# Feed-forward's second product: w_out's high and low parts side by side in one 512-column stream, halves added on eviction, and the bound on |h| found without GpSimd

## The chip, the cores and the metric

The kernel runs on one core of a Trainium2 chip (trn2). The metric is the time of one execution in device microseconds (us); lower is better. Engines: TensorE (PE, its weight loads PEld), VectorE (DVE), ScalarE (ACT), GpSimd (POOL) and the DMA queues (SP's among them).

## The reference, cut to what matters

The kernel computes three layers in turn. Only the last, the feed-forward layer, is touched.

```python
x = fourier_filter(x)                      # 8 x 3072 rows of 256 features -> 24576 tokens
x = mixture_of_experts(x)                  # one expert of 8 per token, 256 -> 1024 -> 256
h = x @ w_in                               # 24576 x 256  @  256 x 2048
g = h - np.tanh(h)
out = g @ w_out                            # 24576 x 2048 @ 2048 x 256, all float32
```

## The kernel before

**Precision.** An operand is split into a high and a low part in a rounded 32-bit format (fp32r, F32R in the code), and a product is the sum of three: high by high, high by low, low by high. x and w_in have parts xh, xl and wih, wil; g has gh, gl; w_out lies in `wo` as 128 x 16 x 2 x 256: for each of 16 blocks f of 128 hidden features first its high part (index 0), then its low part (index 1), 256 columns each.

**Tiling.** `ff_phase` takes the 24576 tokens in NT = 48 tiles of TM = 512, and each tile in 16 steps f. Step f of a tile has these parts:

- `up(X, f)`: six matmuls of 512 columns make h (128 hidden features x 512 tokens) in one PSUM bank of the pool `hp` (4 buffers).
- `small(h)`: ScalarE squares h to u (L1006) and makes s from u (L1007); VectorE makes s = (s + KAPPA) * u (L1008) and g = s * h (L1009). This is h - tanh(h) without its last factor Q3[2], for |h| up to SMALL.
- `parts(g)`: ScalarE rounds g to gh (L998), GpSimd subtracts to gl (L999).
- `down(f, g, po)`: for each of four groups a of 128 tokens three matmuls of 256 columns: gh with wo's high part, gh with its low part, gl with its high part (L1034), each with a weight load of its own. All three add into the same 128 x 256 piece of PSUM. `po` is two tiles of 128 x 2 x 256, a bank each, of the pool `op` (4 buffers), so two token tiles have room.
- after f = 15 `store`: ScalarE copies the two banks to SBUF with the factor Q3[2] (`ob`, L1040), and GpSimd issues four indirect DMAs of 128 rows to the output (L1043), one a step.

**Order.** The order on every engine is that of the program. In turn k of the loop over all 768 (t, f) come `up` and `small` of step k, `parts` of step k-1, then `down` of step k - LAG (LAG = 4), and one pending output DMA. TensorE's order is thus one `up`, one `down`, one `up`, and so on.

**The bound.** The series in `small` holds for |h| up to 0.15. `column_sums` (four times in tile NT-3) adds |w_in| over its two halves. `limit` (before step (NT-2, 0)) sums that over the partitions with four matmuls into buffers of `hp` (L968), takes their maxima on VectorE (L969), reduces them and the maxima of |x| over the 128 partitions on GpSimd (`partition_all_reduce`, L974) and multiplies. If the bound is exceeded, a general loop at the end computes all of it again; with these inputs it is skipped.

Of the kernel before, what the change touches and what calls it, by code (L numbers as in the profile page):

```python
# [16 lines left out]
F32 = mybir.dt.float32  # L17
# [9 lines left out]
D = 256  # L27
# [26 lines left out]
def flat(t):  # L54
    return t.rearrange("p a b -> p (a b)")
# [876 lines left out]
def ff_phase(tc, x2T, ids, out, weights, mx, N, X0):  # L932

    nc = tc.nc
    wih, wil, wo = weights
    NT = N // TM
    with ExitStack() as es:
        P = lambda name, bufs, **kw: es.enter_context(tc.tile_pool(name=name, bufs=bufs, reuse_waits="tile", **kw))
        cp = P("gc", 1)
        beta = cp.tile([128, 1], F32, name="beta")  # L940
        nc.vector.memset(beta, BETA)
        xp = P("gx", 2)
        tp = P("gt", 3)
        hp = P("gh", 4, space=PSUM, side="right")
        op = P("go", 4, space=PSUM)
        one = cp.tile([128, 128], F32, name="gone")
        nc.vector.memset(one, 1.0)
        ones = cp.tile([128, 128], F32R, name="gones")
        nc.scalar.activation(ones, one, AF.Copy)
        big = cp.tile([1, 1], F32, name="big")  # L950
        bigi = cp.tile([1, 1], I32, name="bigi")

        lm = cp.tile([128, 4], F32, name="lm")
        l1 = cp.tile([128, FF], F32R, name="l1")

        def column_sums(q):

            c = slice(TM * q, TM * q + TM)
            a = [cp.tile([128, TM], F32, name=f"abs{k}") for k in range(2)]
            for k in range(2):  # L960
                nc.scalar.activation(a[k], wih[:, k, c].bitcast(F32), AF.Abs)
            nc.vector.tensor_tensor(l1[:, c], *a, op=ALU.add)

        def limit():

            for q in range(4):
                t = hp.tile([128, TM], F32, name="h")
                nc.tensor.matmul(t, ones, l1[:, TM * q : TM * q + TM], start=True, stop=True)  # L968
                nc.vector.tensor_reduce(lm[:, q : q + 1], t, axis=AX.X, op=ALU.max)  # L969
            bound = cp.tile([128, 2], F32, name="bound")  # L970
            nc.vector.tensor_reduce(bound[:, 0:1], lm, axis=AX.X, op=ALU.max)
            nc.vector.tensor_reduce(bound[:, 1:2], mx, axis=AX.X, op=ALU.max)
            allmax = cp.tile([128, 2], F32, name="allmax")
            nc.gpsimd.partition_all_reduce(allmax, bound, 128, bass.bass_isa.ReduceOp.max)  # L974
            nc.vector.tensor_tensor(big, allmax[:1, 0:1], allmax[:1, 1:2], op=ALU.mult)
            nc.vector.tensor_scalar(big, big, 0.99 * SMALL, None, op0=ALU.is_le)
            nc.vector.tensor_scalar(bigi, big, -1.0, 1.0, op0=ALU.mult, op1=ALU.add)

        def load(c):
            steps, X = ff_load(tc, xp, 2, nc.sync, x2T, ids, c)  # L980
            for f in steps:
                f()
            return X

        def up(X, f):
            h = hp.tile([128, TM], F32, name="h")
            c = slice(128 * f, 128 * f + 128)
            n = 0
            for k in range(2):
                for a, b in ((wih, X[0]), (wih, X[1]), (wil, X[0])):  # L990
                    nc.tensor.matmul(h, a[:, k, c], b[:, k], start=n == 0, stop=n == 5)  # L991
                    n += 1
            return h

        def parts(g):
            gh = tp.tile([128, TM], F32R, name="gh")
            gl = tp.tile([128, TM], F32R, name="gl")
            nc.scalar.activation(gh, g, AF.Copy)  # L998
            nc.gpsimd.tensor_tensor(gl, g, gh.bitcast(F32), op=ALU.subtract)  # L999
            return gh, gl  # L1000

        def small(h):
            u = tp.tile([128, TM], F32, name="u")
            s = tp.tile([128, TM], F32, name="s")
            g = tp.tile([128, TM], F32, name="g")
            nc.scalar.activation(u, h, AF.Square)  # L1006
            nc.scalar.activation(s, u, AF.Square, bias=beta)  # L1007
            nc.vector.scalar_tensor_tensor(s, s, KAPPA, u, op0=ALU.add, op1=ALU.mult)  # L1008
            nc.vector.tensor_tensor(g, s, h, op=ALU.mult)  # L1009
            return g  # L1010

        def general(h):
            u = tp.tile([128, TM], F32, name="u")
            s = tp.tile([128, TM], F32, name="s")
            g = tp.tile([128, TM], F32, name="g")
            m = tp.tile([128, TM], I32, name="m", bufs=1)
            t = tp.tile([128, TM], F32, name="t", bufs=1)
            nc.scalar.activation(u, h, AF.Square)
            nc.scalar.activation(t, h, AF.Tanh)
            nc.vector.tensor_scalar(m, u, MID * MID, None, op0=ALU.is_gt)  # L1020
            nc.vector.tensor_tensor(t, h, t, op=ALU.subtract)
            nc.vector.tensor_scalar(u, u, MID * MID, None, op0=ALU.min)
            nc.vector.tensor_scalar(s, u, Q8[7], None, op0=ALU.mult)
            for q in Q8[6::-1]:
                nc.vector.scalar_tensor_tensor(s, s, q, u, op0=ALU.add, op1=ALU.mult)
            nc.vector.tensor_tensor(g, s, h, op=ALU.mult)
            nc.vector.copy_predicated(g, m, t)
            return parts(g)

        def down(f, g, po):  # L1030
            gh, gl = [z.rearrange("p (a n) -> p a n", a=4) for z in g]
            for a in range(4):
                for n, (p, q) in enumerate(((gh, 0), (gh, 1), (gl, 0))):
                    nc.tensor.matmul(po[a // 2][:, a % 2], p[:, a], wo[:, f, q], start=f == 0 and n == 0 and a % 2 == 0,  # L1034
                                     stop=f == 15 and n == 2 and a % 2 == 1)

        def store(ix, po, scale, group):
            ob = [xp.tile([128, 2, D], F32, name="ob", bufs=4) for _ in range(2)]
            for i in range(2):
                nc.scalar.activation(ob[i], po[i], AF.Copy, scale=scale)  # L1040

            def rows(a):
                i = nc.gpsimd.indirect_dma_start(  # L1043
                    out=out, out_offset=bass.IndirectOffsetOnAxis(ap=ix[:, a : a + 1], axis=0),
                    in_=ob[a // 2][:, a % 2], in_offset=None, bounds_check=N - 1, oob_is_err=False)
                if group:
                    tc.declare_no_dep(i.ins, group=group, reason="every token has a row of its own")
                    tc.add_to_no_dep_group(group, i.ins)

            return [lambda a=a: rows(a) for a in range(4)]  # L1050

        seq = [(t, f) for t in range(NT) for f in range(16)]
        X = {0: X0}
        G = {}
        late = []
        LAG = 4
        for k in range(len(seq) + LAG):
            if k < len(seq):
                t, f = seq[k]
                if f == 8 and t + 1 < NT:  # L1060
                    X[t + 1] = load(bass.ds(N - (t + 2) * TM, TM))
                if t == NT - 3 and f % 4 == 2:
                    column_sums(f // 4)
                if (t, f) == (NT - 2, 0):
                    limit()
                G[t, f] = small(up(X[t], f))
            if 0 < k <= len(seq):
                G[seq[k - 1]] = parts(G[seq[k - 1]])
            if k >= LAG:
                t, f = seq[k - LAG]  # L1070
                if f == 0:
                    po = [op.tile([128, 2, D], F32, name="po") for _ in range(2)]
                down(f, G.pop((t, f)), po)
                if f == 15:
                    late = store(X.pop(t)[2], po, Q3[2], "out")
            if late:
                late.pop(0)()
        for f in late:
            f()


        r = nc.values_load(bigi, min_val=0, max_val=1, skip_runtime_bounds_check_because="0 or 1")
        with tc.If(r != 0):
            with tc.For_i(0, N, TM) as i:
                Xi = load(bass.ds(i, TM))
                po = [op.tile([128, 2, D], F32, name="po") for _ in range(2)]
                for f in range(16):
                    down(f, general(up(Xi, f)), po)
                for f in store(Xi[2], po, 1.0, None):
                    f()  # L1090


# [70 lines left out]
```

## Time and profile before

| | us |
|---|---|
| median of 3 runs | 4018.46 |
| lowest and highest run | 4014.62, 4025.91 |
| the profiled execution's own time | 4024.83 |
| its span, first to last instruction | 4023.0 |

The profile records every instruction of one execution. [...] The chain is the work that ended last, followed back from the end. A wait is named by what ended it.

### The profile page before, as it was taken

The page shows a single profiled execution, that of the slowest core. Times are in us where ns is not written, and L with a number is a line of the kernel's source. Part 1 is how long each engine was busy: PE and PEld are TensorE (multiplying, and loading weights), DVE is VectorE, ACT ScalarE, POOL GpSimd, SP SyncE. Part 2 cuts the span into 40 slices and gives each one's busy share as a digit, 9 for nine tenths or more (in the row PEclk, how much of TensorE's full clock was granted, in tenths as well). Part 3 has the DMA queues.
Part 4 walks back from the last instruction along what each step waited for, and adds up shares of the span by engine and source line. Part 5 has one row for each costly group of instructions (what it writes and reads, how often), then busy time and mean ns, then how long its engine had stood idle before and what let it go on. Part 6 is the DMA issues. An engine that isn't in the chain of part 4 may idle for free.

```text
span 4023.0 us, 65752 instructions
## 1 busy us (share of the span) xinstructions
PE 3904.8 (97%) x23204; PEld 3527.1 (88%) x23204; DVE 2621.8 (65%) x4370; ACT 2514.1 (62%) x4318; POOL 2051.7 (51%) x1514
## 2 busy tenths in 40 slices
PE   6899979999999999999999999999999999999998
PEld 3666659999999999999999999999999999999987
DVE  4799986788888877865555555555555555555554
ACT  3455544555555555556777777777777777777775
POOL 2366664344444444444555555555555555555545
PEclk8999999999999999999999999999999999999999
DMA  9898863332333232221000000000001000000000
GB/s 275 264 295 279 270 186 102 76 80 62 77 80 80 55 75 75 54 71 35 22 26 28 22 22 23 26 27 22 22 24 30 22 22 22 26 28 22 22 17 17
DMA packets 297874, 300.13 MB, mean 75 GB/s; under 512 B 158905, under 2 KB 240450, under 8 KB 297538
## 3 DMA queue, kind: packets, MB, share of 16 engines
q1 hardware_dynamic: 275714, 241.83, 21.3%
q0 software_dynamic: 18432, 51.14, 3.5%
q8 instruction: 184, 3.01, 0.3%
q10 hardware_dynamic: 3392, 2.90, 0.2%
q14 instruction: 152, 1.25, 0.1%
HBM read 282.46 MB, written 132.72 MB: 103 GB/s over the span
## 4 chain that ended last, share of the span: by engine, by line
PE 85%; DVE 7%; DMA 4%; issue 2%; POOL 1%; SPq 1%; ACT 1%; POOLq 0%; DVEq 0%; ACTq 0%
PE po L1034 27%; PE h L991 26%; PE h L807 14%; PE o L835 14%; DVE u L261 1%; DVE v L260 1%; DVE v L259 1%; DMA out<-ob,ix 1%; PE z L254 1%; PE z L269 1%; PE z L296 1%; PE L L308 1%; PE z L229 1%; DMA region<-Y,pi 1%; DMA z1d<-a 1%
## 5 line engine op out<-in xcount | busy, mean ns | idle before, releaser
L999 POOL TENSOR_TENSOR gl<-g,gh 128x512 fp32r<-128x512 f32 x768 | 992.9, 1293 | 987.7 <-ACT gh L998 980.4
L1008 DVE SCALAR_TENSOR_TENSOR s<-s,u 128x512 f32<-128x512 f32 x768 | 535.0, 697 | 951.9 <-ACT s L1007 950.1
L1034 PE MATMUL po<-wo,gh 128*128 128x256 f32 x6144 | 1143.0, 282 | 0.0
L1034 PEld LDWEIGHTS po<-wo,gh 128*128 128x128 f32 x6144 | 1007.3, 189 | 71.3
L1034 PE MATMUL po<-wo,gl 128*128 128x256 f32 x3072 | 874.7, 285 | 4.0 <-POOL gl L999 4.0
L1006 ACT ACTIVATE u<-h 128x512 f32<-128x512 f32 x768 | 459.0, 598 | 584.1 <-PE h L991 583.9
L991 PE MATMUL h<-xh,wih 128*128 128x512 f32 x1536 | 610.7, 398 | 0.1
L991 PE MATMUL h<-xl,wih 128*128 128x512 f32 x1536 | 607.6, 396 | 0.0
L991 PE MATMUL h<-xh,wil 128*128 128x512 f32 x1536 | 603.9, 393 | 0.0
L1034 PEld LDWEIGHTS po<-wo,gl 128*128 128x128 f32 x3072 | 581.2, 189 | 4.3 <-POOL gl L999 4.2
L1009 DVE TENSOR_TENSOR g<-s,h 128x512 f32<-128x512 f32 x768 | 529.1, 689 | 84.5 <-POOL gl L999 3.7
L1007 ACT ACTIVATE s<-u,beta 128x512 f32<-128x512 f32 x768 | 554.7, 722 | 25.2
L757 POOL TENSOR_TENSOR w2l<-raw,w2h 128x1024 fp32r<-128x1024 f32 x130 | 349.9, 2692 | 416.7 <-ACT w2h L756 414.4
L817 ACT ACTIVATE hh<-h 128x384 fp32r<-128x384 f32 (+1 forms) x556 | 269.5, 498 | 458.1 <-PE h L807 443.4
L998 ACT ACTIVATE gh<-g 128x512 fp32r<-128x512 f32 x768 | 485.4, 632 | 11.2 <-PE po L1034 4.9
L807 PE MATMUL h<-yh,w1h 128*128 128x384 f32 (+1 forms) x1184 | 392.4, 331 | 10.7 <-DVE hl L818 7.3
L807 PE MATMUL h<-yh,w1l 128*128 128x384 f32 (+1 forms) x1184 | 389.5, 329 | 2.4 <-DVE w1l L757 2.3
L807 PE MATMUL h<-yl,w1h 128*128 128x384 f32 (+1 forms) x1184 | 389.4, 329 | 0.1
L835 PE MATMUL o<-hh,w2h 128*128 128x384 f32 (+1 forms) x1184 | 388.4, 328 | 0.2 <-ACT x L845 0.2
L835 PE MATMUL o<-hl,w2h 128*128 128x384 f32 (+1 forms) x1184 | 388.2, 328 | 0.0
L835 PE MATMUL o<-hh,w2l 128*128 128x384 f32 (+1 forms) x1184 | 388.1, 328 | 0.0
L991 PEld LDWEIGHTS h<-xh,wil 128*128 128x128 f32 x1536 | 288.5, 188 | 71.0
(199 smaller groups left out, 6102.2 us busy)
## 6 DMA issues: line engine op xcount, KB each, us to landing
raw<-in_w SPq DMA_DIRECT2D x260, 512.0 KB
y<-region SPq DMA_DIRECT2D x260, 99.0 KB
x2T<-x SPq DMA_DIRECT2D x65, 384.0 KB
xt<-in_x SPq DMA_DIRECT2D x48, 512.0 KB
z1d<-a SPq DMA_DIRECT2D x96, 256.0 KB
A<-z1d SPq DMA_DIRECT2D x64, 384.0 KB
z3d<-b SPq DMA_DIRECT2D x128, 192.0 KB
bt<-z3d SPq DMA_DIRECT2D x96, 256.0 KB
```

Source lines behind the costliest of these rows:

```text
L757: eng.tensor_tensor(l, r, h.bitcast(F32), op=ALU.subtract)
L807: nc.tensor.matmul(h[j], p[:, k, c], q[:, k], start=n == 0, stop=n == 5)
L817: nc.scalar.activation(oh, t, AF.Relu)
L835: nc.tensor.matmul(O[v][d], p[:, fb, c], q[:, j], start=fb == 0 and n == 0 and (d == 0 or v >= KV), stop=fb == 7 and n == 2 and (d == 1 or ...
L991: nc.tensor.matmul(h, a[:, k, c], b[:, k], start=n == 0, stop=n == 5)
L998: nc.scalar.activation(gh, g, AF.Copy)
L999: nc.gpsimd.tensor_tensor(gl, g, gh.bitcast(F32), op=ALU.subtract)
L1006: nc.scalar.activation(u, h, AF.Square)
L1007: nc.scalar.activation(s, u, AF.Square, bias=beta)
L1008: nc.vector.scalar_tensor_tensor(s, s, KAPPA, u, op0=ALU.add, op1=ALU.mult)
L1009: nc.vector.tensor_tensor(g, s, h, op=ALU.mult)
L1034: nc.tensor.matmul(po[a // 2][:, a % 2], p[:, a], wo[:, f, q], start=f == 0 and n == 0 and a % 2 == 0, stop=f == 15 and n == 2 and a % 2 == 1)
```

## The change

- `down` issues two matmuls per token group instead of three: gh with `flat(wo[:, f])`, 512 columns (high part, then low part) into a whole PSUM bank, and gl with the high part, 256 columns, into the first half of the same bank. `po` is now four tiles of a bank each, all four buffers of `op`.
- A new `sums` evicts: VectorE adds the two halves of a bank with a `tensor_reduce` over a view whose innermost index picks the half (`p (i d) -> p d i`), four a tile. The ScalarE copies (L1040) go. The factor Q3[2] moves into g's VectorE instruction.
- In a turn, `down` and `sums` are now issued between `up` and `small`: on VectorE the four sums stand ahead of step k's s and g.
- The bound's four matmuls and maxima are spread over tile NT-2 (`column_max`, at f = 2, 6, 10, 14), and `limit`, now before step (NT-1, 2), takes the maximum over partitions with VectorE transposes and copies of single rows instead of GpSimd.

```diff
+        def column_max(q):
+            t = hp.tile([128, TM], F32, name="h")
+            nc.tensor.matmul(t, ones, l1[:, TM * q : TM * q + TM], start=True, stop=True)
+            nc.vector.tensor_reduce(lm[:, q : q + 1], t, axis=AX.X, op=ALU.max)
+
         def limit():
-            for q in range(4):
-                t = hp.tile([128, TM], F32, name="h")
-                nc.tensor.matmul(t, ones, l1[:, TM * q : TM * q + TM], start=True, stop=True)
-                nc.vector.tensor_reduce(lm[:, q : q + 1], t, axis=AX.X, op=ALU.max)
-            bound = cp.tile([128, 2], F32, name="bound")
-            nc.vector.tensor_reduce(bound[:, 0:1], lm, axis=AX.X, op=ALU.max)
-            nc.vector.tensor_reduce(bound[:, 1:2], mx, axis=AX.X, op=ALU.max)
-            allmax = cp.tile([128, 2], F32, name="allmax")
-            nc.gpsimd.partition_all_reduce(allmax, bound, 128, bass.bass_isa.ReduceOp.max)
-            nc.vector.tensor_tensor(big, allmax[:1, 0:1], allmax[:1, 1:2], op=ALU.mult)
+            nc.vector.memset(wide, 0.0)
+            nc.vector.tensor_reduce(wide[:, 0:1], mx, axis=AX.X, op=ALU.max)
+            nc.vector.transpose(turned, wide)
+            nc.vector.tensor_reduce(quarter, turned, axis=AX.X, op=ALU.max)
+            nc.vector.tensor_copy(big, quarter[0:1])
+            for p in (32, 64, 96):
+                t = cp.tile([1, 1], F32, name=f"quarter{p}")
+                nc.vector.tensor_copy(t, quarter[p : p + 1])
+                nc.vector.tensor_tensor(big, big, t, op=ALU.max)
+            bound = cp.tile([1, 1], F32, name="bound")
+            nc.vector.tensor_reduce(bound, lm[0:1], axis=AX.X, op=ALU.max)
+            nc.vector.tensor_tensor(big, big, bound, op=ALU.mult)
...
-            nc.vector.tensor_tensor(g, s, h, op=ALU.mult)
+            nc.vector.scalar_tensor_tensor(g, s, Q3[2], h, op0=ALU.mult, op1=ALU.mult)
...
             for a in range(4):
-                for n, (p, q) in enumerate(((gh, 0), (gh, 1), (gl, 0))):
-                    nc.tensor.matmul(po[a // 2][:, a % 2], p[:, a], wo[:, f, q], start=f == 0 and n == 0 and a % 2 == 0,
-                                     stop=f == 15 and n == 2 and a % 2 == 1)
-
-        def store(ix, po, scale, group):
-            ob = [xp.tile([128, 2, D], F32, name="ob", bufs=4) for _ in range(2)]
-            for i in range(2):
-                nc.scalar.activation(ob[i], po[i], AF.Copy, scale=scale)
+                nc.tensor.matmul(po[a], gh[:, a], flat(wo[:, f]), start=f == 0, stop=False)
+                nc.tensor.matmul(po[a][:, :D], gl[:, a], wo[:, f, 0], start=False, stop=f == 15)
+
+        def sums(po):
+            ob = [xp.tile([128, D], F32, name="ob", bufs=8) for _ in range(4)]
+            for o, p in zip(ob, po):
+                nc.vector.tensor_reduce(o, p.rearrange("p (i d) -> p d i", i=2), axis=AX.X, op=ALU.add)
+            return ob
...
-                if (t, f) == (NT - 2, 0):
+                if t == NT - 2 and f % 4 == 2:
+                    column_max(f // 4)
+                if (t, f) == (NT - 1, 2):
                     limit()
-                G[t, f] = small(up(X[t], f))
+                h = up(X[t], f)
+            if k >= LAG:
+                j, f = seq[k - LAG]
+                if f == 0:
+                    po = [op.tile([128, TM], F32, name="po") for _ in range(4)]
+                down(f, G.pop((j, f)), po)
+                if f == 15:
+                    late = store(X.pop(j)[2], sums(po), "out")
+            if k < len(seq):
+                G[seq[k]] = small(h)
             if 0 < k <= len(seq):
                 G[seq[k - 1]] = parts(G[seq[k - 1]])
-            if k >= LAG:
-                t, f = seq[k - LAG]
-                if f == 0:
-                    po = [op.tile([128, 2, D], F32, name="po") for _ in range(2)]
-                down(f, G.pop((t, f)), po)
-                if f == 15:
-                    late = store(X.pop(t)[2], po, Q3[2], "out")
```

## Rows read from the trace of the kernel before

**Rows 1.** The page: busy time by engine, and shares of the chain that ended last.

```profile
PE 3904.8 (97%) x23204; PEld 3527.1 (88%) x23204; DVE 2621.8 (65%) x4370; ACT 2514.1 (62%) x4318; POOL 2051.7 (51%) x1514
...
PE 85%; DVE 7%; DMA 4%; issue 2%; POOL 1%; SPq 1%; ACT 1%; POOLq 0%; DVEq 0%; ACTq 0%
```

**Rows 2.** Windows: length, busy of PE, PEld, DVE, ACT, POOL; clock; DMA share; GB/s.

```profile
2500.00:2600.00 100.00, 100.00 (x638) 90.59 (x637) 51.16 (x72) 71.44 (x113) 53.32 (x44) 1.00 0.08 22
...
3920.00:3930.00 10.00, 6.58 (x32) 5.99 (x33) 3.14 (x4) 4.26 (x8) 6.80 (x6) 0.83 0.04 13
```

**Rows 3.** Chain of waits in order of time: start, length, line, instructions.

```profile
1749.85 2.08 PE o L835 x12
...
1872.03 1.44 PE po L1034 x12
...
3901.23 1.40 PE h L991 x6
3902.63 1.44 PE po L1034 x12
```

**Rows 4.** Timeline of TensorE: the last four downs, first and last row.

```profile
4005.72 0.40 PE L1034 MATMUL po<-wo,gh 128*128 128x256 f32 x2
...
4011.36 0.27 PE L1034 MATMUL po<-wo,gl 128*128 128x256 f32 x1
```

**Rows 5.** Timelines of the engines: the path of one step.

```profile
2502.12 0.39 PE L991 MATMUL h<-xh,wil 128*128 128x512 f32 x1
2502.35 0.41 PE L1034 MATMUL po<-wo,gh 128*128 128x256 f32 x2
...
2502.55 0.60 ACT L1006 ACTIVATE u<-h 128x512 f32<-128x512 f32 x1 [0.88 <-PE h L991]
...
2503.93 0.69 DVE L1008 SCALAR_TENSOR_TENSOR s<-s,u 128x512 f32<-128x512 f32 x1 [1.35 <-ACT s L1007]
2504.73 0.69 DVE L1009 TENSOR_TENSOR g<-s,h 128x512 f32<-128x512 f32 x1
...
2507.42 1.29 POOL L999 TENSOR_TENSOR gl<-g,gh 128x512 fp32r<-128x512 f32 x1 [1.55 <-ACT gh L998]
```

**Rows 6.** Groups of VectorE by line and form: reductions; busy us, mean ns.

```profile
L969 DVE TENSOR_REDUCE lm<-h 128x1 f32<-128x512 f32 x4 | 2.5, 680 | 0.0
...
L846 DVE TENSOR_REDUCE mx<-x 128x1 f32<-128x768 f32 x65 | 61.7, 949 | 45.0 <-ACT x L845 44.7
...
L370 DVE TENSOR_REDUCE pf<-a 128x8 f32<-128x64 f32 x24 | 6.5, 269 | 0.8
...
L330 DVE TENSOR_REDUCE m<-d 128x8 f32<-128x64 f32 x24 | 5.3, 220 | 0.8
```

**Rows 7.** Timelines of the engines around limit.

```profile
3905.51 0.60 ACT L1006 ACTIVATE u<-h 128x512 f32<-128x512 f32 x1 [0.88 <-PE h L991]
...
3908.30 2.48 DVE L969 TENSOR_REDUCE lm<-h 128x1 f32<-128x512 f32 x4
...
3914.79 0.37 POOL L974 PARTITION_ALL_REDUCE allmax<-bound  x1 [5.98 <-issue]
...
3915.38 0.14 DVE L976 TENSOR_SCALAR big<-big 1x1 f32<-1x1 f32 x1
3915.56 0.14 DVE L977 TENSOR_SCALAR bigi<-big 1x1 int32<-1x1 f32 x1
...
3922.12 5.56 POOL L999 TENSOR_TENSOR gl<-g,gh 128x512 fp32r<-128x512 f32 x4 [6.95 <-issue]
...
3923.43 0.51 PE L1034 MATMUL po<-wo,gl 128*128 128x256 f32 x1 [3.99 <-POOL gl L999]
...
3927.84 0.60 ACT L1006 ACTIVATE u<-h 128x512 f32<-128x512 f32 x1 [0.55 <-PE h L991]
```

**Rows 8.** Timelines of ScalarE and GpSimd at the end.

```profile
4010.96 1.31 ACT L1040 ACTIVATE ob<-po 128x512 f32<-128x512 f32 x2 [2.88 <-PE po L1034]
...
4011.83 0.99 POOL L1043 DMA_INDIRECT out<-ob,ix  x1 [2.39 <-ACT ob L1040]
```

More of the change, by code (lines that the diff above doesn't have):

```diff
@@ L962, in column_sums @@
             nc.vector.tensor_tensor(l1[:, c], *a, op=ALU.add)
+        def column_max(q):
+            t = hp.tile([128, TM], F32, name="h")
+            nc.tensor.matmul(t, ones, l1[:, TM * q : TM * q + TM], start=True, stop=True)
+            nc.vector.tensor_reduce(lm[:, q : q + 1], t, axis=AX.X, op=ALU.max)
         def limit():
-            for q in range(4):
-                t = hp.tile([128, TM], F32, name="h")
-                nc.tensor.matmul(t, ones, l1[:, TM * q : TM * q + TM], start=True, stop=True)
-                nc.vector.tensor_reduce(lm[:, q : q + 1], t, axis=AX.X, op=ALU.max)
-            bound = cp.tile([128, 2], F32, name="bound")
-            nc.vector.tensor_reduce(bound[:, 0:1], lm, axis=AX.X, op=ALU.max)
-            nc.vector.tensor_reduce(bound[:, 1:2], mx, axis=AX.X, op=ALU.max)
-            allmax = cp.tile([128, 2], F32, name="allmax")
-            nc.gpsimd.partition_all_reduce(allmax, bound, 128, bass.bass_isa.ReduceOp.max)
-            nc.vector.tensor_tensor(big, allmax[:1, 0:1], allmax[:1, 1:2], op=ALU.mult)
+            wide = cp.tile([128, 32], F32, name="wide")
+            turned = cp.tile([128, 32], F32, name="turned")
+            quarter = cp.tile([128, 1], F32, name="quarter")
+            nc.vector.memset(wide, 0.0)
[10 more added lines that the diff above has]
+            nc.vector.tensor_tensor(big, big, bound, op=ALU.mult)
             nc.vector.tensor_scalar(big, big, 0.99 * SMALL, None, op0=ALU.is_le)
@@ L1032, in down, with store @@
             for a in range(4):
-                for n, (p, q) in enumerate(((gh, 0), (gh, 1), (gl, 0))):
-                    nc.tensor.matmul(po[a // 2][:, a % 2], p[:, a], wo[:, f, q], start=f == 0 and n == 0 and a % 2 == 0,
-                                     stop=f == 15 and n == 2 and a % 2 == 1)
-        def store(ix, po, scale, group):
-            ob = [xp.tile([128, 2, D], F32, name="ob", bufs=4) for _ in range(2)]
-            for i in range(2):
-                nc.scalar.activation(ob[i], po[i], AF.Copy, scale=scale)
+                nc.tensor.matmul(po[a], gh[:, a], flat(wo[:, f]), start=f == 0, stop=False)
[5 more added lines that the diff above has]
+            return ob
+        def store(ix, ob, group):
             def rows(a):
@@ L1044, in rows @@
                     out=out, out_offset=bass.IndirectOffsetOnAxis(ap=ix[:, a : a + 1], axis=0),
-                    in_=ob[a // 2][:, a % 2], in_offset=None, bounds_check=N - 1, oob_is_err=False)
+                    in_=ob[a], in_offset=None, bounds_check=N - 1, oob_is_err=False)
                 if group:
@@ L1085, in ff_phase @@
                 Xi = load(bass.ds(i, TM))
-                po = [op.tile([128, 2, D], F32, name="po") for _ in range(2)]
+                po = [op.tile([128, TM], F32, name="po") for _ in range(4)]
                 for f in range(16):
                     down(f, general(up(Xi, f)), po)
-                for f in store(Xi[2], po, 1.0, None):
+                for f in store(Xi[2], sums(po), None):
                     f()
```

## The prediction

> **What bounds the kernel now.** I read the page first: TensorE is busy for 97% of the span and holds 85% of the chain that ended last [rows 1]. [...] The chain in order of time gives the pace: `down` takes 1.44 us, `up` 1.40, and between the `down` at 1872.03 and the one at 3902.63 lie 2030.6 us, which is 715.0 steps of 2.84 us [rows 3]. So over 715 steps, tile borders included, TensorE never waited: only a change in what it streams, or a new wait, moves this stretch. Behind it comes one place where it does wait, `limit` [rows 7], and then the end.
>
> **The narrower matmuls.** A 256-column matmul costs 0.120 us: 1.44 for 12 [rows 3], and the last four downs, 48 of them with no `up` between, run from 4005.72 to the 48th start at 4011.36, again 0.120 each [rows 4]. A 512-column matmul of the same number format, each with a fresh weight load, costs 1.40 / 6 = 0.2333 us [rows 3]. Twelve narrow ones become four wide and four narrow: 4 x (0.2333 + 0.120) = 1.413 us. The step falls by 0.0267 us to 2.813, and 768 steps by 20.5 us. The columns streamed stay the same (3072 a step); only the cost of a matmul beyond its columns is saved. The wide price is the disputed one, so it is bounded on both sides. Below: the experts' 384-column matmuls take 2.08 / 12 = 0.1733 [rows 3], so the columns from 256 to 384 cost 0.0533, and the same again gives 0.2267 for 512; the saving is then 41 us. Above: a wide one costs as much as two narrow ones, 0.240; the saving is nothing. I take 0.2333, since it is a row of the very width.
>
> **The sums at a tile's border.** Before, two tiles had room in `op`; now the next tile's first `down` needs the four banks that VectorE is still reading. Count from the moment at which the last `down` of a tile has streamed. Group a is complete at -(3 - a) x 0.353, so the first at -1.06; a reader starts 0.20 after the stream (the `up` ends at 2502.35, u starts at 2502.55 [rows 5]), so the first sum can start at -0.86. VectorE is free: g ends 3.07 after its `up` (2504.73 + 0.69 - 2502.35 [rows 5]), and the last `up` whose g stands ahead of the sums ended at -4.23 (1.41 + 1.40 + 1.41), which gives -1.16. The nearest row for a sum is the maximum over a 512-column PSUM bank, four in 2.48 us [rows 6, 7]: the fourth sum ends at 1.62. TensorE follows a release by about 0.02 (the first of four gl ends near 3923.41, the matmul starts at 3923.43 [rows 7]). TensorE first does an `up` (1.40) and reaches group 3 at 1.40 + 3 x 0.353 = 2.46. The margin is 0.8 us, so the sums cost nothing as long as each takes at most 0.2 us more than 0.68. That is the weak point, because this row reads one bank in order, and the sum reads it in steps of 256 elements. The only pair of rows that shows a stride is two reductions of 64 elements to 8 in SBUF: in order 220 ns, with a step of 8 elements 269 [rows 6], which is 0.77 ns more per element. On 512 elements that is 0.39 us a sum. As an upper end each element pays its time twice: a reduction grows by (949 - 680) / 256 = 1.05 ns per element [rows 6], 0.54 us a sum. The lower end is no cost at all. I take no cost, as the rows with a stride are of SBUF and the row of PSUM has none, but keep both ends.
>
> [...]
>
> **What waits behind the sums.** On VectorE, s and g of step k start at 1.62 instead of 0.17 (1.58 after their `up`), 1.45 us late; then gh and gl. gl ends 6.36 after its `up` (2507.42 + 1.29 - 2502.35 [rows 5]) and is needed after four more steps, at 11.25: 4.9 us of slack take it. VectorE works 1.4 of 2.8 us a step [rows 5], so it has caught up a step later. The output DMAs wait for `ob`, which now is ready earlier in the turn than before. ScalarE loses two copies a tile and g's instruction takes one more factor at the same form as s (0.69 both [rows 5]): nothing, neither is on the path.
>
> **The bound.** Around `limit`, u starts behind its `up` at 3905.51 and, five steps later, at 3927.84 [rows 7]: 22.33 us instead of 14.20, so 8.13 us are lost. [...] All but the four matmuls goes: 7.2 us. Each new maximum (0.68) falls in a VectorE gap. One h buffer less for three steps costs nothing, since h is free 3.07 us after its `up` and asked for 7.0 after. The new `limit` is 15 small VectorE instructions at 0.18 each (3915.38 to 3915.56 [rows 7]), 2.7 us between g of step 1 and s of step 2 of the last tile; the sums of the next turn then start 1.1 us late and end 0.3 us after TensorE wants the last bank, once. Bounds for the whole: 6 to 8 us.
>
> **The end.** The last down's first group is summed while the others stream; the first output DMA needs one sum of 0.68 where it needed a copy of 0.6 of two groups [rows 8]. Within 0.3 us.
>
> **Sum.** 20.5 + 7.2 = 27.7, less 0.3: 27.4 us. From the profiled execution's 4024.83 (span 4023.0, 1.8 around it) this gives 3997.4. That execution lies 6.4 above the median 4018.46; from the median it is 3991.
>
> **Rivals.**
>
> *The strided sums make TensorE wait (slower side).* Place: the first `down` of each of 47 tiles. With 0.39 us more a sum the fourth ends at 3.19, 0.75 after it is due: 47 x 0.75 = 35 us, and the time is 4026. With 0.54 more the wait is 1.34 us, 63 us in all, and the time 4054. It eats the whole gain once a sum takes 0.35 us more (1.03 in all). For it: the pair of strided rows. Against: they are of SBUF, in another size. 28 in 100, half of it ending over 0.3% above before.
>
> *The width saves little or nothing.* If a matmul's time went by its columns, 0.120 per 256, a wide one would cost 0.240, and only `limit` is left: 4011. Against: the 512-column row is 0.2333 [rows 3]. 10 in 100.
>
> [...]
>
> *The width saves more.* At 0.2267 the time is 3971. For it: the 384-column row. Against: the row of the very width. 7 in 100.
>
> **How the numbers follow.** The forecast has 55 in 100, with a range of its own of 3983 to 3999 (the bound's 6 to 8 us and the runs' own spread of 0.3%, which is also about what a measurement here can tell from no change). Over all cases the range is 3978 to 4030: above it lies the worse half of the strided rival, below it most of the case that saves more. Faster by over 0.3%: the forecast, the case that saves more and 4 of the 10 of little width, 66 in 100. Within 0.3%: the other 6 and the milder half of the strided sums, 20. Slower: 14.
>
> **What would show it.** Right: `down` in 1.41 us as eight matmuls, starts 0.233 and 0.120 apart; steps of 2.81 across the borders; four sums in about 2.5 us; no GpSimd idle of 6 us and no clock below 1.00 in the last tiles. Wrong: a wait of TensorE on the sums at each tile's first `down`, sums of 1 us or more, or wide matmuls 0.24 apart.

## The result and the profile after

| | before | after |
|---|---|---|
| time, median of 4 runs | 4016.63 us (4014.62 to 4025.91) | 3974.31 us (3968.82 to 3978.37) |
| ratio | | 0.9882, 95% interval 0.9870 to 0.9894 |
| profiled execution, its time / its span | 4024.83 / 4023.0 us | 3977.88 / 3976.1 us |

The kernel is 1.2% faster. The forecast was 3991 and its range began at 3978, so the time lies 4 us below the range. Between the profiled executions the fall is 46.95 us where 27.4 were forecast. In the chains the first `up` of the feed-forward starts at 1822.66 us before and at 1822.76 after, so the whole fall lies in the feed-forward. The page after, the lines of [rows 1]:

```profile
PE 3867.6 (97%) x20132; PEld 3358.8 (84%) x20132; DVE 2760.7 (69%) x4572; ACT 2445.9 (62%) x4222; POOL 2068.9 (52%) x1513
...
PE 86%; DVE 8%; DMA 4%; issue 1%; POOL 1%; ACT 0%; SPq 0%; DVEq 0%; POOLq 0%; ACTq 0%
```

23204 - 20132 = 3072 matmuls are gone, four in each of 768 steps, and TensorE still sets the end. The chain of waits in order of time gives the pace, as [rows 3] did:

```profile
1859.00 1.39 PE h L1003 x6
...
2497.14 1.39 PE h L1003 x6
...
3739.99 1.39 PE h L1003 x6
```

1880.99 us lie between the first row and the last, 675 steps of 2.787 us, borders of tiles included. Before, a step took 2.840. A step is 0.053 us shorter, twice the forecast 0.0267, and over 768 steps that makes 41 us. One step in TensorE's timeline:

```profile
2499.77 0.40 PE L1003 MATMUL h<-xh,wih 128*128 128x512 f32 x1
...
2501.15 0.39 PE L1046 MATMUL po<-wo,gh 128*128 128x512 f32 x1
2501.38 0.28 PE L1047 MATMUL po<-wo,gl 128*128 128x256 f32 x1
2501.49 0.40 PE L1046 MATMUL po<-wo,gh 128*128 128x512 f32 x1
...
2502.55 0.40 PE L1003 MATMUL h<-xh,wih 128*128 128x512 f32 x1
```

The records overlap (the wide matmul at 2501.15 lasts 0.39 us, the next start is 0.23 later), so a pace is read from start to start. A pair of a wide and a narrow matmul takes 0.34 to 0.36 us; 0.353 was forecast. `up`, which the change leaves alone, became shorter too: 1.39 us in the chain, 1.40 in [rows 3]. No step of the prediction has a term for that.

**The sums** do what the forecast said and not what its dearest rival feared. First the group over the feed-forward, then one border of tiles in VectorE's timeline, then in TensorE's (the `up` behind the last `down`, and group 3 of the next `down`):

```profile
L1052 DVE TENSOR_REDUCE ob<-po 128x256 f32<-128x512 f32 x192 | 119.3, 683 | 14.6 <-PE po L1047 14.6
```

```profile
2496.12 2.48 DVE L1052 TENSOR_REDUCE ob<-po 128x256 f32<-128x512 f32 x4 [0.26 <-PE po L1047]
```

```profile
2496.98 0.40 PE L1003 MATMUL h<-xh,wih 128*128 128x512 f32 x1
...
2499.42 0.40 PE L1046 MATMUL po<-wo,gh 128*128 128x512 f32 x1
```

A sum takes 683 ns, and the maximum over a bank in order took 680 [rows 6]: the step of 256 elements added 3 ns. Counted as the prediction counts, from the moment at which the next `up` starts in the timeline (2496.98), the first sum starts at -0.86 and the fourth ends at 1.62, both as forecast, and TensorE reaches group 3 at 2.44 (forecast 2.46).

**The limit**, in the timelines of VectorE, GpSimd and TensorE, and TensorE's weight loads:

```profile
3922.54 0.15 DVE L984 TENSOR_TENSOR big<-big,quarter 1x1 f32<-1x1 f32 x1
...
3922.79 1.15 DVE L987 TENSOR_TENSOR big<-big,bound 1x1 f32<-1x1 f32 x1
3923.97 0.14 DVE L988 TENSOR_SCALAR big<-big 1x1 f32<-1x1 f32 x1
...
3925.60 2.48 DVE L1052 TENSOR_REDUCE ob<-po 128x256 f32<-128x512 f32 x4
```

```profile
3922.64 1.29 POOL L1011 TENSOR_TENSOR gl<-g,gh 128x512 fp32r<-128x512 f32 x1 [1.49 <-ACT gh L1010]
```

```profile
3924.63 0.40 PE L1003 MATMUL h<-xh,wih 128*128 128x512 f32 x1
...
3928.59 0.39 PE L1003 MATMUL h<-xh,wih 128*128 128x512 f32 x1
```

```profile
3926.93 0.19 PEld L1046 LDWEIGHTS po<-wo,gh 128*128 128x128 f32 x1 [0.24 <-DVE ob L1052]
...
3927.53 0.19 PEld L1046 LDWEIGHTS po<-wo,gh 128*128 128x128 f32 x1 [0.30 <-DVE ob L1052]
...
3928.13 0.19 PEld L1046 LDWEIGHTS po<-wo,gh 128*128 128x128 f32 x1 [0.30 <-DVE ob L1052]
```

The window of [rows 2] around it (length, busy time of PE, PEld, DVE, ACT, POOL, clock, DMA share, GB/s):

```profile
3920.00:3930.00 10.00, 9.75 (x46) 7.35 (x45) 9.37 (x25) 5.49 (x9) 4.72 (x4) 1.00 0.04 13
```

GpSimd's 6 and 7 us of [rows 7] are gone, and so is the clock of 0.83: it is 1.00. But the turn from one `up` to the next takes 3.96 us instead of 2.79, since the sums start 0.97 after the start of `up` where 0.86 *before* it is usual. TensorE loses 1.17 us, where 0.3 was forecast; only 0.25 of that shows as idle time, the rest as weight loads that start 0.6 us apart, each released by a sum.

### The profile page after: what moved, and what is told of

Same layout as the page of the kernel before. It is cut to its first block, busy times and chain, and to the rows that moved or that the text cites. A ratio compares the mean times of both kernels' runs of the same rounds, so it can differ in the third digit from the quotient of the medians.

```text
span 3976.1 us, 59852 instructions
## 1 busy us (share of the span) xinstructions
PE 3867.6 (97%) x20132; PEld 3358.8 (84%) x20132; DVE 2760.7 (69%) x4572; ACT 2445.9 (62%) x4222; POOL 2068.9 (52%) x1513
## 4 chain that ended last, share of the span: by engine, by line
PE 86%; DVE 8%; DMA 4%; issue 1%; POOL 1%; ACT 0%; SPq 0%; DVEq 0%; POOLq 0%; ACTq 0%
PE h L1003 26%; PE po L1046 18%; PE h L807 14%; PE o L835 14%; PE po L1047 9%; DVE u L261 1%; DVE v L259 1%; DVE v L260 1%; DMA out<-ob,ix 1%; PE z L254 1%; PE z L269 1%; PE z L296 1%; DMA A<-z1d 1%; PE L L308 1%; DMA z1d<-a 1%
## 5 line engine op out<-in xcount | busy, mean ns | idle before, releaser
L1046 PE MATMUL po<-wo,gh 128*128 128x512 f32 x3072 | 1113.2, 396 | 0.2 <-ACT gh L1010 0.2
L1020 DVE SCALAR_TENSOR_TENSOR s<-s,u 128x512 f32<-128x512 f32 x768 | 553.4, 721 | 770.6 <-ACT s L1019 768.7
L1047 PE MATMUL po<-wo,gl 128*128 128x256 f32 x3072 | 861.0, 280 | 0.0
L1046 PEld LDWEIGHTS po<-wo,gh 128*128 128x128 f32 x3072 | 577.2, 188 | 136.6 <-DVE ob L1052 0.8
L1021 DVE SCALAR_TENSOR_TENSOR g<-s,h 128x512 f32<-128x512 f32 x768 | 529.0, 689 | 81.1 <-DVE s L1020 1.9
L1003 PEld LDWEIGHTS h<-xh,wih 128*128 128x128 f32 x1536 | 288.3, 188 | 72.1
```

The lines of the kernel that those rows point to most:

```text
L1021: nc.vector.scalar_tensor_tensor(g, s, Q3[2], h, op0=ALU.mult, op1=ALU.mult)
L1046: nc.tensor.matmul(po[a], gh[:, a], flat(wo[:, f]), start=f == 0, stop=False)
L1047: nc.tensor.matmul(po[a][:, :D], gl[:, a], wo[:, f, 0], start=False, stop=f == 15)
```

## The experiments

Ratios are to the kernel before on the same chip, with a 95% interval where a kernel ran more than once; a step is read from the chain of waits, (last start - first start) / steps between.

### One part of the change at a time

`narrow_down` gives each `down` its three narrow matmuls back, still into one bank with the sums:

```diff
-                matmul(po[a], gh[:, a], flat(wo[:, f]), ...)
+                for q in range(2):
+                    matmul(po[a][:, D * q : D * q + D], gh[:, a], wo[:, f, q], ...)
```

> The changed kernel with only the width undone: gh goes against w_out's high part and its low part in two matmuls of 256 columns, into the two halves of the same bank; sums, order and bound stay as changed. [...] Rival 'price of the row': a wide matmul costs 0.2333 us, and the rest of the measured saving came from the new order or from the eviction: step 2.787 -> 2.813, time 3995.

`narrow_up` leaves `down` as changed and cuts each matmul of `up` in two halves of 256 columns, six matmuls more a step:

```diff
-                    matmul(h, a[:, k, c], b[:, k], ...)
+                    for i in range(2):
+                        d = slice(256 * i, 256 * i + 256)
+                        matmul(h[:, d], a[:, k, c], b[:, k, d], ...)
```

> The changed kernel with up's six matmuls of 512 columns split into twelve of 256, nothing else. [...] 'Price of the row' (0.2333 against 2 x 0.120): 6 x 6.7 = 40 ns, step 2.827, time 4005.

Chain of waits of `narrow_down` (20 steps between the rows), then of `narrow_up` (20 steps):

```profile
2730.39 1.39 PE h L1003 x6
...
2786.78 1.39 PE h L1003 x6
```

```profile
2730.63 1.43 PE h L1005 x12
...
2787.70 1.43 PE h L1005 x12
```

`narrow_down`: a step of 2.820 us, ratio 0.9949 (0.9933 to 0.9966). `narrow_up`: 2.853, ratio 1.0005 (0.9994 to 1.0015). The prices of the rows, 0.2333 and 0.120, give 2.813 and 2.827: neither step is theirs. The surprise is `narrow_down`: it streams what the kernel before streams, in as many matmuls, and yet its step is 0.020 us below 2.840. Something other than the width is 20 ns of the 53.

`bound_only` is the kernel before with nothing but the new bound:

```diff
+        def column_max(q): ...
         def limit(): (as in the change)
...
-                if (t, f) == (NT - 2, 0):
+                if t == NT - 2 and f % 4 == 2:
+                    column_max(f // 4)
+                if (t, f) == (NT - 1, 2):
                     limit()
```

> The kernel before with only the bound without GpSimd: column_max in tile NT-2, limit with VectorE transposes before step (NT-1, 2). Theory: of the 8.13 us lost around limit only the four matmuls (0.93) stay, steps of 2.84 as before: 4016.6 - 7.2 = 4009. Rival: GpSimd's idle time was hidden or the new chain takes its place: 4016.

```profile
2731.95 1.43 PE po L1046 x12
...
2796.81 1.43 PE po L1046 x12
```

Ratio 0.9936 (0.9916 to 0.9955): 26 us saved where the bound was to bring 7. These 23 steps take 2.820 each in its chain, and no instruction of a step differs from before. At `limit` TensorE is busy throughout, as the window of `bound_only` around it shows, so the bound's own 8.13 - 0.93 = 7.2 us are what was forecast (0.93 for its four matmuls of 512 columns, at the 0.2333 of [rows 3]). The other 768 x 0.020 = 15.4 us come in every step.

```profile
3930.00:3950.00 20.00, 20.00 (x129) 18.16 (x128) 12.98 (x30) 13.34 (x23) 9.15 (x8) 1.00 0.00 1
```

`old_order` puts `small` ahead of `down` and `sums` again, so that s and g stand ahead of the four sums:

```diff
-                h = up(X[t], f)
+                G[t, f] = small(up(X[t], f))
...
-            if k < len(seq):
-                G[seq[k]] = small(h)
```

> The changed kernel with small back in front of down, so that on VectorE the four sums stand behind the step's s and g. Theory: the border has a margin of 0.8 us only because the sums come first. Behind g they start at 1.67 after the last down's stream, the fourth ends at 4.15 and is due at 2.42: TensorE waits 1.73 us at each of 47 borders, 81 us, time 4055. Rival: the banks are free in time in either order, time 3974.

TensorE's timeline at one border of `old_order`:

```profile
1912.45 0.39 PE L1003 MATMUL h<-xh,wih 128*128 128x512 f32 x1
...
1914.88 0.47 PE L1046 MATMUL po<-wo,gh 128*128 128x512 f32 x1 [0.88 <-DVE ob L1052]
...
1917.03 0.39 PE L1003 MATMUL h<-xh,wih 128*128 128x512 f32 x1
```

4.58 us from `up` to `up` instead of 2.79: 1.8 us lost at each border, ratio 1.0075 (1.0055 to 1.0095). The order of issue is what makes the sums free; the margin that the prediction counted was real.

### Do the buffers' places set the pace?

What `bound_only` and `narrow_down` share is `limit`'s small tiles. They lie in SBUF ahead of the buffers of x and of g's parts: two of 128 bytes per partition and five of one column, 32 bytes each, in place of two of 32, so those buffers start 352 bytes later (in the programs' own addresses the first gh goes from 86912 to 87264, xh from 43904 to 44256, and the weights stay). The tests put in tiles that nothing uses.

```diff
         lm = ...
+        cp.tile([128, n // 4], F32, name="pad")
```

`before_pad352` is the kernel before with n = 352, `before_pad32` with 32.

> The kernel before with one unused tile of 352 bytes a partition in the pool gc, in front of the pools that hold x's and g's parts; not one instruction changes. It is by how much the new bound's tiles move those buffers. Theory 'place': TensorE's pace depends on where in SBUF its operands start, so the step falls from 2.840 to 2.820 us as it did with the new bound alone, and the time by 768 x 0.020 = 15 us, 4018 -> 4003, with limit's loss of 8.1 us unchanged. Rival 'bound': the pace came from the new bound's instructions; then 2.840 and 4018.

> The kernel before with an unused tile of 32 bytes at the same place. Theory 'place', by the odd or even multiple of 32 bytes alone: 2.820 us a step and 4003, as with 352. If a larger unit decides (352 and 32 differ from 64 bytes on), the step is another one: 2.840 and 4018 would say that 32 bytes alone do nothing.

`after_pad160` is the changed kernel with n = 160, which makes 352 into 512; `after_all0` has 160 there and 32 more behind `wo`.

> The changed kernel with an unused tile of 160 bytes at the same place, which with the 352 makes 512: x's and g's parts start where they did before, up to multiples of 512 bytes. Theory 'place': the step rises by up to what the place gave, 2.787 -> 2.807 us, time 3974 + 15 = 3989; less if wide matmuls pay less for it. Rival: the place matters only with narrow matmuls, 2.787 and 3974.

> As the run before, and w_in's and w_out's parts moved by 32 bytes too, so that all six operands of TensorE start at even multiples of 32 bytes. If what counts is that stationary and moving operand start alike, the step is 2.787 us again, time 3974; if even places are bad by themselves, 2.807 or more, 3989.

Chain of waits of `before_pad352` (24 steps):

```profile
2730.94 1.43 PE po L1035 x12
...
2798.62 1.43 PE po L1035 x12
```

An unused tile makes the kernel before faster: a step of 2.820 instead of 2.840, ratio 0.9960 (0.9945 to 0.9974). That is the step of `bound_only` and `narrow_down`. `before_pad32`: 2.813, ratio 0.9951 (0.9935 to 0.9968). `after_pad160`: 2.800, ratio 0.9902 (0.9886 to 0.9919); its step is longer than the changed kernel's 2.787 by the unused tile alone, while the intervals of the two ratios overlap. `after_all0`: 2.807, ratio 0.9911 (0.9891 to 0.9932); so the weights' place counts too.

### Which places, and with which period

The scans give x's parts, g's parts or both another start in each tile of tokens, 32 bytes further each time, so that one run holds 48 starts:

```diff
-     xh = pool.tile([128, 2, TM], ...)
+     xh = pool.tile([128, 2 * TM + 512], ...)[:, off : off + 2 * TM]
-            gh = tp.tile([128, TM], ...)
+            gh = tp.tile([128, TM + 512], ...)[:, off : off + TM]
```

(off = 8 * t elements for tile t; xl and gl alike.) `scan_both` moves all four in the changed kernel, `scan_x` and `scan_g` one pair, `scan_narrow` all four in the kernel before, and `scan_grid` x by the tile's number modulo 8 and g by its number divided by 8.

> The changed kernel, but in token tile t the parts of x and of g (xh, xl, gh, gl) start 32 t bytes further into a buffer with room for it; every other buffer keeps its place up to multiples of 2048 bytes. Theory 'place': TensorE's pace depends on where the operands start that it reads, so the step changes from tile to tile, between about 2.78 and 2.81 us as in the padded kernels, and the tiles in which the places come out as in a padded kernel have its step (t = 5, 160 bytes: 2.800). Rival: the padding worked through the buffers of the other engines (u, s, g, ob), which moved with it; then all tiles run at 2.787.

> As the run before, with x's parts alone moved by 32 t bytes (moving operand of up). If x's place counts, the step changes from tile to tile; before, the first tile, whose x lies elsewhere, ran at 2.827 and the others at 2.840, so a change of some 0.01 us is expected. Rival: only g's place counts; 2.787 in all tiles.

> As the run before the last, with g's parts alone moved by 32 t bytes (stationary operand of down). If g's place counts, the step changes from tile to tile by some 0.01 us. Rival: only x's place counts; 2.787 in all tiles.

> The kernel before with x's and g's parts moved by 32 t bytes in token tile t. Theory 'place': its step too changes with a period of 8 tiles, 256 bytes; t = 0, 8, ... at 2.840, t = 1, 9, ... (32 bytes) at 2.813 and t = 3, 11, ... (96 bytes, which is the place of the kernel with 352) at 2.820. If the width saves 13 ns a matmul at any place, the mean over the eight places is 2.845, 53 ns above the 2.792 of the wide kernel; if it saves 6.7 ns, the price of the row, 2.819.

> The changed kernel with x's parts moved by 32 (t mod 8) bytes and g's by 32 (t div 8): 48 pairs of places. If the two places act each for itself, the step is 2.787 plus what x's place adds alone (0 to 0.020) plus what g's place adds alone (-0.020 to 0.026): for g at 96 bytes and x at 0, 2.780. The scan of both at once speaks against it (at 128 bytes 2.767 where the two alone add 0.004), so pairs off by 0.01 or more are expected.

Two places from the chain of `scan_narrow`, 8 steps each: its own place in tile 8, then 160 bytes further in tile 13.

```profile
2202.04 1.40 PE h L991 x6
...
2224.76 1.40 PE h L991 x6
...
2426.98 1.37 PE h L991 x6
...
2449.06 1.37 PE h L991 x6
```

2.840 and 2.760 us for the same 18 matmuls. All four scans repeat after 256 bytes: the column 0 of the table is read 256 bytes on, in tile 8, and gives the 2.840 and 2.787 of the unmoved kernels to 0.001. Each ran once, and its tiles are compared with each other; the mean granted clock of the four was 0.987 to 0.989 (0.990 in the trace of before). Steps in us by bytes moved, each the mean of 8 steps of the chain and good to about 0.002:

| moved by | 0 | 32 | 64 | 96 | 128 | 160 | 192 | 224 |
|---|---|---|---|---|---|---|---|---|
| `scan_narrow` (from the place before) | 2.840 | 2.814 | 2.800 | 2.820 | 2.806 | 2.760 | 2.820 | 2.825 |
| `scan_both` (from the place after) | 2.786 | 2.794 | 2.786 | 2.794 | 2.768 | 2.800 | 2.806 | 2.800 |
| `scan_x` | 2.788 | 2.786 | 2.786 | 2.803 | 2.791 | 2.786 | 2.806 | 2.788 |
| `scan_g` | 2.788 | 2.794 | 2.814 | 2.780 | 2.786 | 2.796 | 2.780 | 2.768 |

The table gives the other kernels' steps. 352 is 256 + 96: `before_pad352`, `bound_only` and `narrow_down` stand at 96 in the first line (2.820), `before_pad32` at 32 (2.813), `after_pad160` at 160 in the second (2.800). The kernel before happened to lie at the worst of its eight places. In `scan_grid` the sum of what x and g do alone misses by 10 ns or more at 19 of the 34 pairs in which both are moved (tile NT-2, with the bound's matmuls, left out): it is the two places together that matter.

Two more things can be read from these traces. The first is from where a place counts. In the programs' own addresses the tile behind `wo` moves the weights 32 bytes down and leaves x's and g's parts alone, so that these lie 32 bytes further from the weights in `after_all0` than in `after_pad160`. Its step is that of `scan_both` at 160 + 32 = 192 (2.807 and 2.806), and on the mean the 14 matmuls of a step start at the same distances as there, to within 1 ns; each of the other seven places of `scan_both` misses one of these distances by more than 6 ns. So, as far as one such run shows, what counts is where x's and g's parts lie relative to the weights.

The second is who takes part. At the end of a trace four `down` follow each other with no `up` between them, and for a while VectorE, ScalarE and GpSimd have nothing to do. Two rows of TensorE's timeline there and a window (as [rows 2]), of the kernel before and of `narrow_best`, a kernel of the next section that has these instructions at another place:

```profile
4009.68 0.40 PE L1034 MATMUL po<-wo,gh 128*128 128x256 f32 x2
...
4010.76 0.40 PE L1034 MATMUL po<-wo,gh 128*128 128x256 f32 x2
4009.50:4010.90 1.40, 1.40 (x14) 1.40 (x14) 0.00 (x0) 0.00 (x0) 0.00 (x0) 1.00 0.02 6
```

```profile
3937.73 0.39 PE L1047 MATMUL po<-wo,gh 128*128 128x256 f32 x2
...
3938.41 0.39 PE L1047 MATMUL po<-wo,gh 128*128 128x256 f32 x2
3937.50:3938.60 1.10, 1.10 (x12) 1.10 (x11) 0.00 (x0) 0.00 (x0) 0.00 (x0) 1.00 0.00 0
```

Nine starts in 1.08 us are 0.120 each, six in 0.68 are 0.113. The difference between the places is there with those three engines idle, so in `down` at least it does not need them; that it lies between TensorE's own accesses is the author's estimate (DMA was busy for 0.02 of the first window and 0.00 of the second).

### Is it the change between up and down? And the best of each

`pairs` issues two `up` and then two `down`, half as many changes from one to the other, with `limit` ahead of step (NT-1, 8):

```diff
-        for k in range(len(seq) + LAG):
+        for k in range(0, len(seq) + LAG, 2):
...
-                h = up(X[t], f)
+                h = [up(X[t], f + i) for i in range(2)]
```

> The changed kernel with two ups and then two downs in a turn, instead of one and one, and limit before step (NT-1, 8), away from the sums. If part of what a step takes beyond its columns falls at the change from up to down and back, half of these changes are gone and the step falls, by up to 0.02 us, 15 us in all: 3959. If it lies in the matmuls themselves, 2.787 as before and 3973, only limit's wait of about 1 us gone.

2.797 a step and a ratio of 0.9907 (0.9878 to 0.9936): no gain, so there is no sign of a price per change. The order also changes which reads follow each other, which this run does not separate.

`pad128_late` is the changed kernel with n = 128 and `limit` away from the sums:

```diff
+        cp.tile([128, 32], F32, name="pad")
...
-                if (t, f) == (NT - 1, 2):
+                if (t, f) == (NT - 1, 8):
```

`narrow_best` is `bound_only` with n = 64: 352 + 64 is 256 + 160, the best place of `scan_narrow`. `pad128_again` is `pad128_late` beside it on the same chip.

> The changed kernel with an unused tile of 128 bytes in front of x's and g's buffers, the place that had the lowest step when both moved (2.767 us), and limit before step (NT-1, 8) instead of (NT-1, 2). Theory 'place': step 2.787 -> 2.767, 15.4 us, and the wait of 1.2 us at limit gone: 3974 - 16.6 = 3958. Rival: the low step came with buffers of varying place only; 3973.

> The kernel before (narrow matmuls, sums of halves not needed, ScalarE evicts) with the bound without GpSimd and an unused tile of 64 bytes, which together put x's and g's parts 416 bytes further, in steps of 256 the same as 160: the narrow kernel's lowest step in the scan, 2.760 us. Theory 'place': 768 x (2.820 - 2.760) = 46 us under the same kernel without the 64 bytes (3997): 3951, below every wide kernel so far. Rival: the wide matmuls are what makes the changed kernel fast, and this one stays above it: 3974 or more.

> The wide kernel at its lowest place, the same file as in pad128_late, as the neighbour on the same chip: 2.767 a step, 3966 again. Theory 'place': the narrow kernel beside it is faster by up to 768 x 0.007 = 5 us. Rival: the wide one is faster.

Chain of waits of `pad128_late` (21 steps), then of `narrow_best` (24 steps):

```profile
2730.56 1.38 PE h L1004 x6
...
2788.66 1.38 PE h L1004 x6
```

```profile
2730.79 1.39 PE po L1047 x12
...
2797.03 1.39 PE po L1047 x12
```

| kernel | matmuls of `down` | step, us | median, us | ratio |
|---|---|---|---|---|
| the change | 4 wide, 4 narrow | 2.787 | 3974.31 | 0.9882 (0.9870 to 0.9894) |
| `pad128_late` | 4 wide, 4 narrow | 2.767 | 3966.02 | 0.9849 (0.9835 to 0.9862) |
| `pad128_again` | 4 wide, 4 narrow | 2.767 | 3957.32 | 0.9847 (0.9834 to 0.9861) |
| `narrow_best` | 12 narrow | 2.760 | 3954.80 | 0.9838 (0.9825 to 0.9852) |

Both versions beat the changed kernel, and with each at the best place that was found, twelve narrow matmuls are as fast as eight of mixed width: the intervals of their ratios overlap. `pad128_late` and its repeat ran on two chips, on which the kernel before took 4026.33 and 4020.87 us; their ratios agree.

## Why the prediction was wrong

**Where the fall came from.** In the order place, then width, then bound: 2.840 to 2.820 by the place (15.4 us, forecast nothing); 2.820 to 2.787 at that place by the width (0.0333 x 768 = 25.6 us, forecast 20.5); `limit` 8.13 - 0.93 - 1.17 = 6.0 us (forecast 6.9 with the 0.3 taken off). Together 47.0 of the 46.95 measured. In the other order the width comes first, at the place before, and is worth 40 ns a step there (2.840 to `after_pad160`'s 2.800), the place 13: place and width do not simply add.

**The step that failed** is in "What bounds the kernel now": "only a change in what it streams, or a new wait, moves this stretch". A third thing does: where the operands lie in SBUF. `limit`'s new tiles moved them, and "The bound" has no term for it. `before_pad352` shows it, with an unused tile and nothing else: 2.820 us a step for 2.840. The trace of before could have raised the doubt, in two places of its chain of waits that lie outside [rows 3]:

```profile
1822.66 6.81 PE h L991 x30
...
1832.45 1.43 PE po L1034 x12
...
1863.56 1.44 PE po L1034 x12
```

Thirty matmuls of `up` in a row took 0.227 us each, not 0.2333; and in the first tile of tokens the 11 steps between the last two rows take 2.828 each, not 2.840 (the first tile's x lies in a buffer of its own, at another place). The same instructions at two paces, without a wait, say that a row's price holds for its own circumstances.

**The narrower matmuls.** Form and sign were right at this place, and 25.6 us lies within the bounds given (0 to 41). But the step took 0.2333 and 0.120 for the prices of a matmul. They are the prices at one place, the worst of eight. With the operands at equal places, `scan_narrow` less `scan_both` (96 bytes shift one line of the table against the other) gives 40, 8, 0, 34, 12, -26, 26 and 57 ns a step: 19 on the mean, 14.6 us in all, and a loss at one place. The mean is of the size of the forecast's 26.7, but what the width is worth at a single place is no property of the width alone.

**Sums, order, end.** All as forecast, within 0.02 us at each point of the border; `old_order` lost 1.8 us a border without the new order. From the first output DMA (3964.98) to the end of the span it is 11.1 us, 11.2 before.

**The bound.** GpSimd's part was sized right: 8.13 less the 0.93 of the four matmuls is the 7.2 of the sum, and in `bound_only` TensorE is busy throughout around `limit`. The 15 instructions took 3.6 us and not 2.7, since one of them, L987, took 1.15 instead of 0.15; s and the sums came late behind it, and TensorE lost 1.17 us where 0.3 was forecast: a term mis-sized by 0.9.

**The rivals.** The strided sums fell: 683 ns against the 1.03 us from which they decide. The pair of rows that spoke for them, 220 and 269 ns, differs in the operation too (a maximum and a sum), so it never showed the stride alone. "The width saves little" fell at this place, though at others it would have held. That 4 of its 10 chances would come out over 0.3% faster rests on no row: what the width was worth went from -26 to 57 ns a step with the place. "The width saves more" has the nearest time (3971) for the wrong reason: not 53 ns a step by the width, but 33 by the width and 20 by the place.

**What stays open.** Whether accesses of TensorE meet at a bad place, and which, and why the period is 256 bytes: the moving operand and the weights of the next matmul were not told apart, and for `up` the other engines are not ruled out. Nor is the place all: `old_order` has the changed kernel's places, and of its tiles most odd ones run at 2.780 a step and most even ones at 2.787. The buffers of u, s, g and `ob` are ruled out as the cause inside a scan, since they kept their places from tile to tile.

## What to carry to other kernels

With TensorE busy throughout, its pace still moved here by 2.9 per cent (2.760 to 2.840 us a step) with the place of its operands in SBUF; before a gain of that size is credited to an edit, run the old kernel with an unused tile that moves its buffers as the edit does. Scan the places first (one run does it, with another start in each tile of tokens) and compare each version at its best place: here the best place was worth about as much to the narrow kernel (ratio 0.9936 to 0.9838) as the whole change (to 0.9882). In a stretch that waits for nothing, a pace that differs between two passages of the same instructions is a row to explain before the price goes into a sum.

## What the runs showed of the hardware

- TensorE's step of 18 matmuls took 2.760 to 2.840 us by the start of x's and g's parts modulo 256 bytes (`scan_narrow`, mean granted clock 0.987), without a wait. With VectorE, ScalarE and GpSimd idle, a matmul of 256 columns took 0.120 us at one place and 0.113 at another.
- A VectorE instruction on two single elements lasted until GpSimd's gl had ended: L987 in the changed kernel from 3922.79 to 3923.94, gl to 3923.93. In `pairs`, where `limit` meets gl elsewhere, it is another of the two-input instructions, and again it ends with gl (3954.90 and 3954.89), while the copy ahead of it, under the same gl, took 0.14:

```profile
3953.75 0.14 DVE L983 COPY quarter<-quarter 1x1 f32<-1x1 f32 x1
3953.93 0.97 DVE L984 TENSOR_TENSOR big<-big,quarter 1x1 f32<-1x1 f32 x1
3954.91 0.14 DVE L983 COPY quarter<-quarter 1x1 f32<-1x1 f32 x1
```

```profile
3953.59 1.30 POOL L1011 TENSOR_TENSOR gl<-g,gh 128x512 fp32r<-128x512 f32 x1 [2.15 <-PE po L1046]
```

- A reduction over two PSUM elements 256 apart cost VectorE 683 ns and one over a bank in order 680, while in SBUF a sum in steps of 8 elements cost 269 and a maximum in order 220 [rows 6].
